# One more pair of tiles 2 to 17 computed as a split product, with a written order for the first phase and the first 24 tiles

## The chip, the cores and the metric

The kernel runs on one core of one Trainium2 chip. The metric is device time in microseconds, from one execution of the whole program; lower is better. TensorE does the matmuls, VectorE (DVE), ScalarE (ACT) and GpSimd (POOL) the elementwise work, and the queue of SyncE (SP) issues all the DMAs.

## The reference

Two batches of 12480 tokens with 128 channels, 49 agents, 2048 hidden units, all float32:

```python
agent_v = softmax(scale * agents @ k.T) @ v          # per batch, 49 x 128
x       = softmax(scale * q @ agents.T) @ agent_v    # per batch, 12480 x 128
h       = x @ w_in                                   # 24960 x 2048
g       = where(h >= 1, h, where(h <= -1, 0, (h + 1)**2 / 4))
out     = g @ w_out                                  # 24960 x 128
```

The product `agent_v @ w_in` is formed once for each batch, so `h` of a token is its 49 softmax weights times a 49 x 2048 matrix.

## The kernel before

**Tiles.** The 24960 tokens are cut into 49 tiles of 512 tokens (the last has 384). The 2048 hidden units of a tile are handled as 8 pairs of two blocks of 128. For each pair: `g1` (L2025, TensorE) computes `h` into PSUM (`ph`); ACT makes `relu(0.5 h + 0.5)` (L2033) and squares it (L2038); DVE forms `g = max(min(g, 1), h)` (`gate`, L2041).

**Second product.** `g @ w_out` is then done in one of two ways, by a letter per pair:
- N, a plain float32 pair: `g` is multiplied directly by the float32 weights (`g2n`, `total<-g,wo` at L2071).
- D, A or P, a split pair: `g` is rounded to a float32r tile `ghi` (the "hi" step, on DVE at L1089, ACT at L1085 or POOL at L1087), the rest `glo = g - ghi` is formed (the "lo" step, L2052, on DVE or POOL by a second letter), and three products are added: `ghi,wo_hi`, `ghi,wo_lo` and `glo,wo_hi`, all at L2071.

Both accumulate in two PSUM banks, `total0` and `total1`, one for each half of the rows. When all pairs of a tile are in, ACT copies bank 0 (`out`), DVE adds bank 1 (`join`, L2151), and SP stores the tile.

Tiles 0 to 17 have the letters `DPNPNDPP` / `PPDDDPDD` (two plain pairs, 2 and 4). Tiles 18 to 48 alternate `PPNPNDPP` / `PPPPDPDD` (two plain) and `PAPPNPDD` / `DDDPDDPP` (one plain).

**Queries.** For each tile (for two tiles together from tile 18 on) the scores `q @ agents` (L1879), their softmax (DVE and ACT; `pq` at L1912 is the last step), a transpose (`tr`, L1938) and two drains of it (`mc` on ACT at L1085, `ml` on DVE at L1948) make the small matrix `mt` that `g1` reads.

**First phase.** Before tile 0's second product, the keys and values of batch 0 are loaded and reduced, the weights are decoded from 64-bit words (L1176 to L1212) and `W` of batch 0 is formed. The keys of batch 1 (14 groups) are scored early into the banks `total0` and `total1` (L1128); each group is copied to `ks` by ACT or DVE and folded by DVE into a running maximum `top` (L1660), which ends in one reduction (L1691). Tile 0's second product needs these banks back. The values of batch 1 are weighted later, as riders on the query scores of tiles 5 to 12 (L1136; the subtraction is L1742 on POOL), and `W` of batch 1 is formed on those of tiles 13 to 17.

**Order.** A planner (`Order.run`) puts all steps into one order before the program is written out, with assumed durations; each engine then works through its own list in that order. Steps of the tiles have turns (tile number plus an entry of `TIMES`, `TIMES_2` or `PLAN`), and follow each other by turn on DVE, ACT and TensorE. `PLAN` has entries of their own for tiles 13 to 21 and 44 to 48; other tiles share `TIMES` (0 to 12) or the two of `TIMES_2`. The remaining steps (first phase, riders, DMAs, the queries of tiles 0 to 2) go greedily, whichever can start first, by a key; `FIRST` ranks 473 of them. Buffers limit it: three `ph` banks, five each of `g`, `ghi` and `glo`.

Of the kernel before, what the change touches and what calls it, by code (L numbers as in the profile page):

```python
# [11 lines left out]
AHEAD = 0.8  # L12
# [23 lines left out]

TIMES = dict(  # L40
    q=(-1.8875417,),
    mx=(-0.3865384,),
    sub=(-0.3146318,),
    exp=(-2.1729306,),
    tot=(0.1808175,),
    rec=(0.4518768,),
    norm=(0.4759488,),
    tr=(-0.1276526,),
    mc=(-1.0964621,),
    ml=(1.1333586,),  # L50
    out=(0.9032897,),
    join=(3.1102148,),
    g1=(0.0668635, 0.4000499, 0.1916538, 0.0411721, 0.8964628, 0.9435512, 0.9732315, 0.5142120),
    relu=(-0.5071955, -0.1941977, -0.4279925, -0.7025724, -0.0055905, 0.0340225, 0.2099995, -0.1183292),
    square=(-0.4804701, -0.1725691, -0.2858129, -0.5818398, 0.0945863, 0.1749406, 0.2375538, -0.0976778),
    gate=(1.6527569, 2.0147262, 1.9982946, 1.5815822, 2.2200233, 2.2700605, 2.5717267, 2.1086864),
    hi=(1.9175717, 2.5099120, None, 1.9817459, None, 2.5080745, 2.9293395, 2.4146834),
    lo=(2.3736696, 2.6831976, None, 1.9174717, None, 2.7685071, 2.6705867, 2.1491229),
    g2=(1.0521998, 1.5614394, 0.9499837, 1.0285587, 1.0875494, 1.4817716, 1.6962020, 0.9785378),
    g2l=(1.3136540, 1.7077630, None, 1.2353176, None, 1.8013004, 1.7208422, 1.3753477),  # L60
)

PAIRS = 18
QUERY = ("q", "mx", "sub", "exp", "tot", "rec", "norm")
HI_2 = ("PPNPNDPP", "PAPPNPDD")
LO_2 = ("PPPPDPDD", "DDDPDDPP")
TIMES_2 = (
    dict(  # L70
        q=(-1.5713,),
        mx=(-0.5974,),
        sub=(-0.5235,),
        exp=(-0.1685,),
        tot=(0.0236,),
        rec=(1.3849,),
        norm=(1.4461,),
        tr=(0.8994,),
        mc=(2.3488,),
        ml=(2.2710,),  # L80
        out=(4.4525,),
        join=(4.3718,),
        g1=(1.6621, 1.4877, 1.9336, 2.1986, 2.4419, 2.5160, 2.2733, 1.2761,),
        relu=(3.0360, 2.8721, 3.1890, 3.3281, 3.8045, 3.8312, 3.7296, 2.7669,),
        square=(3.3034, 3.1553, 3.3145, 3.3684, 3.8260, 3.9316, 3.7952, 2.8452,),
        gate=(3.1999, 3.0999, 3.2210, 3.2325, 3.4800, 3.7033, 3.3712, 2.7199,),
        hi=(62.3857, 62.0442, None, 62.5259, None, 3.7501, 62.7598, 61.8730,),
        lo=(62.6767, 62.2078, None, 62.7896, None, 62.8395, 3.7723, 3.1606,),
        g2=(2.7027, 2.4767, 2.5185, 2.8430, 2.8277, 3.0118, 2.9034, 2.5554,),
        g2l=(2.9002, 2.5015, None, 2.8840, None, 3.1268, 2.9103, 2.7007,),  # L90
    ),
    dict(
        tr=(1.2661,),
        mc=(2.6113,),
        ml=(2.2934,),
        out=(4.7847,),
        join=(4.3181,),
        g1=(2.2479, 1.8295, 1.5940, 1.5287, 2.4567, 2.1755, 1.8336, 1.7939,),
        relu=(3.6045, 3.1881, 3.0018, 2.9632, 3.8472, 3.5778, 3.2527, 3.1117,),
        square=(3.8312, 3.3162, 3.0897, 2.9701, 3.8503, 3.7077, 3.3291, 3.1391,),  # L100
        gate=(3.7103, 3.0976, 2.9045, 2.7898, 3.9433, 3.5896, 3.1374, 2.9799,),
        hi=(62.7859, 3.4148, 61.9105, 61.9524, None, 62.5856, 3.4494, 3.0235,),
        lo=(4.0405, 3.5378, 2.9935, 62.0055, None, 3.8415, 62.3033, 62.0323,),
        g2=(2.9416, 2.6801, 2.3409, 2.3085, 3.2104, 3.0125, 2.4289, 2.3251,),
        g2l=(3.2075, 2.6861, 2.4733, 2.4846, None, 3.2923, 3.3724, 2.6053,),
    ),
)
PLAN = {
    13: dict(
        q=(-1.8875,),  # L110
        mx=(-0.3303,),
        sub=(-0.2435,),
        exp=(-2.0215,),
        tot=(0.2512,),
        rec=(0.4553,),
        norm=(0.6044,),
        tr=(-0.1505,),
        mc=(-1.0807,),
        ml=(1.1437,),
        g1=(  # L120
            0.0661, 0.2927, 0.2186, 0.0309,
            0.8249, 0.8521, 1.0696, 0.5431,
        ),
        relu=(
            -0.5630, -0.3641, -0.4949, -0.7518,
            -0.0200, 0.1707, 0.3731, -0.1859,
        ),
        square=(
            -0.5050, -0.2158, -0.3273, -0.7210,
            0.1039, 0.3272, 0.3999, -0.1026,  # L130
        ),
        gate=(
            1.6537, 1.9476, 1.8362, 1.6224,
            2.1550, 2.4118, 2.5022, 2.0639,
        ),
        hi=(
            2.0137, 3.5040, None, 2.0680,
            None, 2.4627, 4.3563, 2.9470,
        ),
        lo=(  # L140
            2.5714, 3.5050, None, 1.7949,
            None, 3.9050, 2.8465, 2.4354,
        ),
        g2=(
            1.2684, 1.5254, 1.0404, 0.8654,
            1.1496, 1.7221, 1.4987, 1.0531,
        ),
        g2l=(
            1.4845, 1.6689, None, 1.4204,
            None, 1.9048, 1.8506, 1.5448,  # L150
        ),
        out=(0.9856,),
        join=(3.1582,),
    ),
    14: dict(
        q=(-1.8674,),
        mx=(-0.3313,),
        sub=(-0.2221,),
        exp=(-2.0994,),
        tot=(0.1109,),  # L160
        rec=(0.1722,),
        norm=(0.5086,),
        tr=(-0.1639,),
        mc=(-0.8055,),
        ml=(1.1705,),
        g1=(
            0.2526, 0.3343, 0.3675, 0.1185,
# [2138 lines left out]
```

## Time and profile before

| | |
|---|---|
| runs, us | 1011.97, 1012.07, 1012.99 (median 1012.07) |
| span of the profiled execution | 1011.9 us (no other time of that execution is recorded) |
| TensorE (PE) busy | 988.7 us, 98% |
| ACT busy | 909.4 us, 90% |
| DVE busy | 882.1 us, 87% |
| POOL busy | 720.9 us, 71% |
| DMA moved | 57.03 MB |
| chain that ended last | PE 78%, ACT 9%, DVE 5%, issue 3%, DMA 2% |

Busy shares are means over stages of different kinds. In the page's 40 slices of 25.3 us the DMA engines are at 90 to 100% in the first two and below 30% from the fourth on; PE reads 7 and 8 tenths in the first two slices, 8 in the last, and 9 or more in all between; TensorE's granted clock reads 9 tenths or more in every slice. The stages have to be read one by one.

### The profile page before, as it was taken

Reading aid. Unit: us, or ns where it says so; the run is one execution under the profiler, and the core shown is the slowest. Engines: PE = TensorE matmul, PEld = TensorE weight load, DVE = VectorE, ACT = ScalarE, POOL = GpSimd, SP = SyncE. Lnnn points to the kernel's source line nnn. Section 1 sums busy time; section 2 is a strip of 40 time slices with the busy share of each in tenths; the row PEclk is TensorE's granted clock in tenths of the full one; section 3 lists DMA queues with packets and bytes.
Section 4 is the critical chain, followed back from the end, with each engine's and each line's share of the span. In section 5 each row is a group of like instructions: output and inputs, shape, how many; then the busy total and the mean of one; then the engine's idle time right before and its main releaser. Section 6 shows DMA issues by size and latency. Waiting matters only on the chain.

```text
span 1011.9 us, 22370 instructions
## 1 busy us (share of the span) xinstructions
PE 988.7 (98%) x9143; PEld 757.3 (75%) x9143; DVE 882.1 (87%) x1008; ACT 909.4 (90%) x1008; POOL 720.9 (71%) x423
## 2 busy tenths in 40 slices
PE   7899999999999999999999999999999999999998
PEld 5767777777777676867778878778777877777777
DVE  7698988887899889889889889889989889988986
ACT  3488988888899889889999999999999999999996
POOL 3536766667566554777877887878878788788785
PEclk9999999999999999999999999999999999999999
DMA  9981021212000101000100100101011010000000
GB/s 352 401 315 37 23 69 59 69 59 68 23 26 29 33 22 43 33 32 12 43 32 12 43 32 12 43 32 35 20 32 42 12 33 30 12 22 12 11 22 19
DMA packets 23862, 57.03 MB, mean 56 GB/s; under 512 B 2768, under 2 KB 3280, under 8 KB 23760
## 3 DMA queue, kind: packets, MB, share of 16 engines
q1 hardware_dynamic: 23760, 55.60, 15.4%
q8 instruction: 72, 1.18, 0.5%
q14 instruction: 30, 0.25, 0.1%
HBM read 42.81 MB, written 12.78 MB: 55 GB/s over the span
## 4 chain that ended last, share of the span: by engine, by line
PE 78%; ACT 9%; DVE 5%; issue 3%; DMA 2%; POOL 1%; SPq 0%; DVEq 0%; ACTq 0%; POOLq 0%
PE total L2071 46%; PE ph L2025 24%; ACT g L2033 5%; ACT g L2038 3%; DVE g L2041 3%; PE ph L1879 3%; PE ph L1938 1%; PE ph L1136 1%; PE total L1136 1%; DMA kbuf<-kT 1%; PE total L2064 1%; DVE glo L2052 1%; DMA g<-kT 1%; DMA qt<-qT 1%; POOL glo L2052 1%
## 5 line engine op out<-in xcount | busy, mean ns | idle before, releaser
L2052 POOL TENSOR_TENSOR glo<-g,ghi 128x1024 fp32r<-128x1024 f32 (+1 forms) x163 | 429.9, 2643 | 155.9 <-DVE ghi L1089 114.6
L2041 DVE SCALAR_TENSOR_TENSOR g<-g,ph 128x1024 f32<-128x1024 f32 (+1 forms) x392 | 467.2, 1210 | 72.5 <-ACT g L2038 54.9
L2033 ACT ACTIVATE g<-ph,half 128x1024 f32<-128x1024 f32 (+1 forms) x392 | 427.8, 1104 | 45.1 <-PE ph L2025 38.5
L2038 ACT ACTIVATE g<-g 128x1024 f32<-128x1024 f32 (+1 forms) x392 | 406.5, 1054 | 6.1
L1087 POOL CAST ghi<-g 128x1024 fp32r<-128x1024 f32 (+1 forms) x212 | 253.9, 1216 | 89.9 <-DVE g L2041 82.2
L2025 PE MATMUL ph<-mt,w_hi 49*128 49x512 f32 (+2 forms) x1600 | 278.4, 420 | 6.7 <-DVE g L2041 6.3
L2071 PE MATMUL total<-ghi,wo_hi 64*128 64x512 f32 x1212 | 198.7, 397 | 0.0
L2025 PEld LDWEIGHTS ph<-mt,w_hi 49*128 49x128 f32 x1600 | 146.7, 185 | 68.4 <-issue 25.4
L2052 DVE TENSOR_TENSOR glo<-g,ghi 128x1024 fp32r<-128x1024 f32 (+1 forms) x146 | 192.8, 1321 | 4.3 <-POOL ghi L1087 2.6
L2071 PE MATMUL total<-ghi,wo_lo 64*128 64x512 f32 x1212 | 195.2, 392 | 0.0
L2071 PE MATMUL total<-glo,wo_hi 64*128 64x512 f32 x1212 | 179.7, 397 | 0.0
L2025 PE MATMUL ph<-mt,w_lo 49*128 49x512 f32 (+2 forms) x800 | 160.9, 386 | 0.0
L2071 PE MATMUL total<-g,wo 64*128 64x512 f32 x648 | 153.8, 589 | 1.4 <-DVE top L1660 1.4
L2071 PEld LDWEIGHTS total<-ghi,wo_hi 64*128 64x128 f32 x1212 | 120.9, 185 | 23.8 <-issue 2.3
L2071 PEld LDWEIGHTS total<-ghi,wo_lo 64*128 64x128 f32 x1212 | 121.1, 184 | 21.7
L2071 PEld LDWEIGHTS total<-glo,wo_hi 64*128 64x128 f32 x1212 | 117.4, 185 | 22.4 <-issue 1.2
L2071 PEld LDWEIGHTS total<-g,wo 64*128 64x128 f32 x648 | 65.2, 185 | 44.0 <-issue 36.8
L2025 PEld LDWEIGHTS ph<-mt,w_lo 49*128 49x128 f32 x800 | 79.6, 185 | 13.9 <-DVE w_lo L1550 0.2
L1089 DVE CAST ghi<-g 128x1024 fp32r<-128x1024 f32 x82 | 66.4, 810 | 1.5
L1879 PEld LDWEIGHTS ph<-ag,qt 128*64 128x64 f32 x780 | 25.7, 137 | 19.7 <-issue 13.1
L2151 DVE TENSOR_TENSOR ot<-ot,total 128x512 f32<-128x512 f32 x48 | 32.8, 684 | 6.8 <-ACT ot L1085 6.5
L1085 ACT ACTIVATE ot<-total 128x512 f32<-128x512 f32 (+1 forms) x49 | 28.6, 585 | 9.6 <-PE total L2064 5.1
(120 smaller groups left out, 559.2 us busy)
## 6 DMA issues: line engine op xcount, KB each, us to landing
qt<-qT SPq DMA_DIRECT2D x48, 256.0 KB, 2.8
outT<-ot SPq DMA_DIRECT2D x48, 256.0 KB, 2.0
vbuf<-v_in SPq DMA_DIRECT2D x18, 451.5 KB, 4.6
kbuf<-kT SPq DMA_DIRECT2D x17, 448.0 KB, 7.5
ghi<-v_in SPq DMA_DIRECT2D x5, 451.5 KB, 8.1
glo<-v_in SPq DMA_DIRECT2D x5, 451.5 KB, 8.1
g<-kT SPq DMA_DIRECT2D x5, 448.0 KB, 9.2
raw<-w_in SPq DMA_DIRECT2D x4, 512.0 KB, 7.0
```

What stands on the lines that cost most here:

```text
L1085: act.activation(out=out, in_=in_, func=ACTF.Copy)
L1087: pool.tensor_copy(out, in_)
L1089: dve.tensor_copy(out, in_)
L1136: nc.tensor.matmul(out=ps[c:c + 64, 0:C + 1], lhsT=ksf[:, g, t * A:t * A + 64], rhs=vt[:, t, :], start=n + t < 2, stop=n + t >= m - 2,)
L1879: nc.tensor.matmul(out=ps[c, m * A:(m + 1) * A], lhsT=st["q", x][:, i * 128:][:, c], rhs=ag[:, b, :], start=True, stop=True,)
L2025: nc.tensor.matmul(out=st["h"][:, c, lo:hi], lhsT=W[b][w][r, f:f + 128], rhs=M[j][r, x, lo:hi], start=(i == 0), stop=(i == 2),)
L2033: act.activation(out=st["g"], in_=st["h"][:, :, 0:n], func=ACTF.Relu, bias=half, scale=0.5)
L2038: act.activation(out=st["g"], in_=st["g"], func=ACTF.Square)
L2041: dve.scalar_tensor_tensor(out=st["g"], in0=st["g"], scalar=1.0, in1=st["h"][:, :, 0:n], op0=ALU.min, op1=ALU.max,)
L2052: (pool if e == "POOL" else dve).tensor_tensor(out=st["lo"], in0=st["g"], in1=st["hi"].bitcast(F32), op=ALU.subtract)
L2071: nc.tensor.matmul(out=tot[i][:, 0:n], lhsT=w[r, f, :], rhs=x[r, c, :], start=begins, stop=LEFT[j] == 0,)
L2151: dve.tensor_tensor(out=st["o"], in0=st["o"], in1=tot[1][:, 0:n], op=ALU.add)
```

## The change

Every step now has a turn, and each engine's list is sorted by turn alone: the planner no longer picks greedily, it only works out the waits. `PLAN` has an entry for each of the 49 tiles, with the query loads (`ld`) and the stores (`st`) in it; `LEAD` gives turns to the 386 steps of the first phase and of the riders; nine of these move to their second engine (`SECOND`). The turns of tiles 24 to 48 put these tiles' steps in the same sequence on TensorE, ACT, DVE and POOL as before.

The letters stand per tile. Pair 4 of tiles 2 to 17 is split instead of plain. Over these 16 tiles the hi steps go from 32 DVE, 64 POOL, 0 ACT to 31 DVE, 70 POOL, 11 ACT, and the lo steps from 48 DVE, 48 POOL to 61 DVE, 51 POOL. Five drains `mc` (tiles 6, 7, 10, 14, 15) and one `out` (tile 12) go from ACT to DVE. Tile 0 has one lo step on DVE and five on POOL instead of three and three; tile 1 has three hi steps on DVE instead of two. Tiles 19, 20, 21 and 23 have one or two letters changed, and the same number of plain pairs.

In the first phase's DMA list, the loads of the keys of batch 0 all stand ahead of its values, with three weight loads and one query load between them (before, two loads of values stood among the keys).

```diff
-HI_ENG = (("DPNPNDPP",), ("DPNPNDPP",))
-LO_ENG = (("PPDDDPDD",), ("PPDDDPDD",))
+CUT = ('DPNPNDPP', 'DPNDNDPP', 'DPNPPDPP', 'DPNAPAPP', 'PDNPPPAD', 'DPNPDPAP', 'PDNPDPPP', ...
+LOW = ('PPDPDPPD', 'PPDDDPDD', 'PPDDDPDD', 'PPDDDPDD', 'PPDDDPDD', 'PPDDDPDD', 'PPDDDPDD', ...
+MC_ON = 'AAAAAADDAADAAADDAAAADAAAAAAAAAAAAAAAAAAAAAAAAAAAA'
+OUT_ON = 'AAAAAAAAAAAADAAAAAAAAADAAAAAAAAAAAAAAAAAAAAAAAAAA'
...
+    def settle(self):
+        rest = [op for op in self.ops if op.turn is None]
+        for op, turn in zip(rest, LEAD):
+            op.turn = turn
+        for i in SECOND:
+            rest[i].choices = rest[i].choices[1:]
...
     def run(self):
+        self.settle()
+        queues = {
+            e: sorted(
+                (op for op in self.ops if op.choices[0][0] == e),
+                key=lambda op: (op.turn, op.n), reverse=True,
+            )
+            for e in self.ENGINES
+        }
...
-            x = add(("ACT", 0.5), hi, [d], k)
-            y = add(("ACT", 0.3), keep, [d], k)
-            wo_ops.append(add(("POOL", 1.3, 1), lo, [x, y], k, (), ((b, d),)))
+            x = add(("ACT", 0.8), hi, [d])
+            wo_ops.append(add(("POOL", 1.3, 1), lo, [x], (), (("wf", d),)))
...
-            x = step("mc", ("ACT", 0.08 + n / 1.2e3), mc, [tr_op], j=j)
+            x = step("mc", drain(MC_ON, j, n), mc, [tr_op], j=j)
```

The rest of the diff renames steps, removes switches that had one setting, shortens the `ks` buffer and the zeroing of its tail, and changes two waits that the planner assumes for DMAs.

## Rows read from the trace of the kernel before

**Rows 1.** Windows: stretch, its length, busy us (instructions) PE, PEld, DVE, ACT, POOL; clock, DMA.

```profile
51.00:78.50 27.50, 23.80 (x444) 17.23 (x444) 27.08 (x47) 23.14 (x36) 11.65 (x10) 1.00 0.80 297
...
116.00:438.00 322.00, 318.71 (x2770) 238.72 (x2769) 282.56 (x334) 287.97 (x315) 202.77 (x125) 1.00 0.13 43
438.00:576.00 138.00, 135.47 (x1222) 105.56 (x1220) 122.21 (x125) 131.75 (x139) 107.16 (x60) 1.00 0.09 30
576.00:997.00 421.00, 420.58 (x3650) 325.71 (x3647) 377.33 (x386) 407.03 (x434) 341.69 (x184) 1.00 0.07 25
```

**Rows 2.** Waits of PE, 78.5 to 560 us: total us, times, longest.

```profile
PE ph L2025 <- DVE g L2041: 5.8, 15, 0.9
```

**Rows 3.** Timeline of PE, 651 to 666 us: start, us, engine line op xcount.

```profile
651.39 0.64 PE L2071 MATMUL total<-ghi,wo_hi 64*128 64x512 f32 x4
...
655.13 0.64 PE L2025 MATMUL ph<-mt,w_hi 49*128 49x512 f32 x4
...
663.88 1.90 PE L2071 MATMUL total<-g,wo 64*128 64x512 f32 x8
665.60 0.54 PE L1938 MATMUL ph<-ident,pq 64*113 64x64 f32 x8
```

**Rows 4.** Instruction groups by form, 116 to 438 us: busy, mean ns, idle before.

```profile
L2038 ACT ACTIVATE g<-g 128x1024 f32<-128x1024 f32 x126 | 131.7, 1057 | 2.4
...
L2052 DVE TENSOR_TENSOR glo<-g,ghi 128x1024 fp32r<-128x1024 f32 x47 | 68.6, 1461 | 2.0 <-POOL ghi L1087 0.9 <-PE total L2071 0.8
L1089 DVE CAST ghi<-g 128x1024 fp32r<-128x1024 f32 x31 | 21.6, 695 | 0.1
L1948 DVE TENSOR_TENSOR mt<-ph,mt 113x512 fp32r<-113x512 f32 x16 | 10.9, 682 | 0.3 <-ACT mt L1085 0.3
...
L1912 DVE TENSOR_TENSOR pq<-qd,qsm 128x392 f32<-128x392 f32 x14 | 8.3, 589 | 0.3
...
L2052 POOL TENSOR_TENSOR glo<-g,ghi 128x1024 fp32r<-128x1024 f32 x48 | 125.7, 2621 | 86.7 <-DVE ghi L1089 77.2 <-PE total L2071 7.4 <-PE ph L2025 1.0
L1087 POOL CAST ghi<-g 128x1024 fp32r<-128x1024 f32 x65 | 70.6, 1111 | 34.3 <-DVE g L2041 31.0 <-PE ph L2025 3.3
L1742 POOL TENSOR_TENSOR ks<-ks,mb 128x343 f32<-128x343 f32 x12 | 10.3, 878 | 0.0
```

**Rows 5.** Timelines of POOL and DVE, 220 to 234 us.

```profile
220.16 2.02 POOL L1087 CAST ghi<-g 128x1024 fp32r<-128x1024 f32 x2 [1.84 <-DVE g L2041]
222.26 3.27 POOL L2052 TENSOR_TENSOR glo<-g,ghi 128x1024 fp32r<-128x1024 f32 x1
227.16 2.38 POOL L2052 TENSOR_TENSOR glo<-g,ghi 128x1024 fp32r<-128x1024 f32 x1 [1.63 <-DVE ghi L1089]
...
221.23 2.02 DVE L2052 TENSOR_TENSOR glo<-g,ghi 128x1024 fp32r<-128x1024 f32 x1
...
233.57 1.22 DVE L2052 TENSOR_TENSOR glo<-g,ghi 128x1024 fp32r<-128x1024 f32 x1
```

**Rows 6.** Instruction groups by form of POOL and DVE, 620 to 860 us.

```profile
L2052 POOL TENSOR_TENSOR glo<-g,ghi 128x1024 fp32r<-128x1024 f32 x45 | 119.0, 2650 | 21.7 <-DVE ghi L1089 12.0 <-PE total L2071 9.2
L1087 POOL CAST ghi<-g 128x1024 fp32r<-128x1024 f32 x60 | 79.0, 1329 | 22.1 <-DVE g L2041 20.7
...
L2052 DVE TENSOR_TENSOR glo<-g,ghi 128x1024 fp32r<-128x1024 f32 x39 | 47.5, 1217 | 0.0
L1089 DVE CAST ghi<-g 128x1024 fp32r<-128x1024 f32 x18 | 16.2, 900 | 0.6
```

**Rows 7.** Timelines of DVE, then PE, in the first phase.

```profile
67.56 1.30 DVE L2052 TENSOR_TENSOR glo<-g,ghi 128x1024 fp32r<-128x1024 f32 x1
...
77.39 0.50 DVE L1089 COPY ks<-total 128x343 f32<-128x343 f32 x1
...
36.01 0.60 PE L1136 MATMUL total<-ghi,ks 128*64 128x129 f32 x6 [1.93 <-issue]
...
78.47 1.95 PE L2071 MATMUL total<-g,wo 64*128 64x512 f32 x7 [1.44 <-DVE top L1660]
```

More of the change, by code (lines that the diff above doesn't have):

```diff
@@ L799, with __init__ @@
 class Op:
-    def __init__(self, order, choices, fn, deps, key, acq, rel):
-        self.choices, self.fn, self.deps, self.key = choices, fn, list(deps), key
+    def __init__(self, n, choices, fn, deps, acq, rel):
+        self.n, self.choices, self.fn, self.deps = n, choices, fn, list(deps)
         self.acq, self.rel = acq, rel
-        self.n = order
-        self.start = self.end = None
+        self.start = self.end = self.engine = None
         self.slots = {}
@@ new lines, in earliest @@
+                at = max(at, stored[op.tile - 1][1] if op.tile else 0.0)
+            if op.reads in seen and seen[op.reads][0] != e:
+                x, end = seen[op.reads]
+                at = max(at, end + latency(x, e))
+            return at
+        while any(queues.values()):
+            best = None
+            for n, queue in enumerate(queues.values()):
+                if not queue:
+                    continue
+                at = earliest(queue[-1])
+                if at is None:
+                    continue
+                e, us, shared = queue[-1].choices[0]
+                c = max(at, free[e], port if shared else 0.0), n, queue
+                if best is None or c[:2] < best[:2]:
+                    best = c
+            assert best is not None, [q[-1].tag for q in queues.values() if q]
+            at, _, queue = best
+            op = queue.pop()
+            e, us, shared = op.choices[0]
@@ L1025, in agent_attention_moe @@
     wo_lo = const.tile([128, NC, 128], F32R, name="wo_lo")
+    native = sorted({p for table in CUT for p in range(NP) if table[p] == "N"})
+    wo = {p: const.tile([128, 2, 128], F32, name=f"wo{p}") for p in native}
     def width(j):
@@ L1485, in keys_phase @@
                 else:
-                    last = add(("DVE", 0.55), halves, [x], k + 1)
+                    last = add(("DVE", 0.55), halves, [x])
         return last, av_ops[1:]
-    W, FORMS = {}, []
+    W = {}
     def plus(ps):
@@ L1524, in n3 @@
             ]
-        x = add(("PE", 0.32), n2, [acc_op], key + 0.1)
+        x = add(("PE", 0.32), n2, [acc_op])
         back = take(x)
-        nx = add(("DVE", 0.2), n3, [x], key + 0.2)
-        r = add(("DVE", 0.26), n1, [nx], key + 0.25, (), (back,))
+        nx = add(("DVE", 0.2), n3, [x])
+        r = add(("DVE", 0.26), n1, [nx], (), (back,))
         done = []
@@ L1553, in lo @@
                 )
-            x = add(("PE", 0.87), form, [nx, win_ops[i]], key + 0.3 + i, ("h",))
-            FORMS.append(x)
-            y = add(("ACT", 0.5), hi, [x, r], key + 1 + i)
-            done.append(add(("DVE", 0.6), lo, [y], key + 1.1 + i, (), (("h", x),)))
+            x = add(("PE", 0.87), form, [nx, win_ops[i]], ("h",))
+            y = add(("ACT", 0.5), hi, [x, r])
+            done.append(add(("DVE", 0.6), lo, [y], (), (("h", x),)))
         return done
@@ L1676, in early @@
             KE[g] = add(
-                (("ACT", 0.355), ("DVE", 0.42)), evac, [y, wait[g]], key + 0.1, (),
+                (("ACT", 0.355), ("DVE", 0.42)), evac, [y, wait[g]], (),
                 () if g and g not in GMP1 else ((lent, x),),
@@ L2119, in pair, with last @@
             x.rows = y.rows = 256
-        SECOND.setdefault(j, []).extend((x, y))
-    def last_g1(j):
-        return max(range(NP), key=lambda p: time("g1", j, p))
-    def last(j, n, *turns):
+        PRODUCTS.setdefault(j, []).extend((x, y))
+    def last(j, n):
         for i, e in enumerate(("ACT", "DVE")):
@@ L2135, in store @@
                 nc.sync.dma_start(out=outT[:, at:at + n // 2], in_=st["o"])
-            x = add((e, 0.06 + n / 1.92e3), evac, SECOND[j], turns[i] * NP, ("o",))
-            x.turn, x.tag = turns[i], (("out", "join")[i], j, 0)
+            x = timed(
+                add((e, 0.06 + n / 1.92e3), evac, PRODUCTS[j], ("o",)), ("out", "join")[i], j
+            )
             x.store = j if i else None
-            load(64 * n * 4, store, [x], turns[i] * NP, (), (("o", x),))
+            timed(load(64 * n * 4, store, [x], (), (("o", x),)), "st", j)
     def output(j):
```

2104 lines of the change are left out of this document (1184 added, 920 removed), and 68 rows, old and new, of tables (FIRST, LEAD).

## The prediction

> **What bounds the kernel now.** Start with the page's shares: TensorE is busy 98% of the span, so the first question is where the other 2% lie, and a mean cannot tell. The table of windows by stage does [rows 1]. From 576 to 997 us PE is busy 420.58 of 421 us: nothing but less TensorE work can shorten that stretch. From 116 to 438 us, in which the outputs of the 16 tiles 2 to 17 end, it is busy 318.71 of 322, and from 438 to 576 us 135.47 of 138. From 51 to 78.5 us PE has slack (23.80 of 27.50), and DVE has none (27.08). So the kernel has two bounds: DVE in the second half of the first phase, TensorE from then on. The list of waits names the TensorE idle behind 78.5 us: 15 waits for `gate`, the DVE step that turns `h` into `g`, 5.8 us in all [rows 2], which is what the two middle windows lack (3.3 + 2.5).
>
> **TensorE: what one more split pair is worth.** In the PE timeline [rows 3] eight groups of four split-product matmuls fill 651.39 to 655.13 us, 0.4675 us for a group. A split pair is three such groups (`ghi,wo_hi`, `ghi,wo_lo`, `glo,wo_hi`): 1.40 us. A plain pair is one row of eight records, 663.88 to 665.60: 1.72 us. Each exchange takes 0.32 us off TensorE, and there are 16: 5.1 us. All of it is on the path as long as PE stays fed, since PE is busy 99% of that stretch [rows 1]. I take -5.1 us; the ends are 0 (it all comes back as waits) and 5.1.
>
> **What the split adds on the other engines.** The 16 new hi steps and 16 new lo steps, with the letters moved, make per engine over tiles 2 to 17:
> - DVE: 13 more lo steps, one hi step less, six drains more. An unblocked lo step is 1.22 us [rows 5], a hi step 0.70, a drain about the 0.68 of `mt` [rows 4]: 15.9 - 0.7 + 4.1 = 19.3 us.
> - ACT: 11 hi steps at the 1.06 of the square, which has the same shape [rows 4]: 11.7 us, less the six drains that leave it.
> - POOL: 3 lo steps at 2.38 and 6 hi steps at 1.01 [rows 5]: 13.2 us.
>
> The stretch would last 322 - 5.1 = 317 us. DVE goes from 282.6 to 301.9 us, 95%; without the time that its lo steps now spend blocked (47 times 1.461 - 1.22, 11.3 us [rows 4]) it is 290.6, 92%. ACT goes to at most 299.7, 95%. POOL, 202.8 + 13.2, has room. In the stretch from 576 to 997 us ACT is at 407.03 of 421, 97%, DVE at 90%, with PE idle 0.4 us [rows 1]: ACT's level has been carried before, DVE's has not quite.
>
> **The two engines are not independent.** POOL's two casts run from 220.16 to 222.18, and the DVE lo step that starts at 221.23 takes 2.02 us instead of 1.22; the POOL lo step behind it starts at 222.26 and takes 3.27 instead of 2.38 [rows 5]. In each case the later one ends about its own length after the earlier one has ended. So I add up these steps as if only one could run at a time. Before, 116 to 438 us [rows 4]: POOL 48 x 2.38 + 65 x 1.01 + 12 x 0.88, DVE 47 x 1.22 + 31 x 0.70 + 14 x 0.59 = 190.5 + 87.3 = 277.8 us, 86% of 322. After: 13 x 1.22 + 3 x 2.38 + 6 x 1.01 - 0.70 = 28.4 us more, 306.2 of 317, 97%. The check is the later stage, 620 to 860 us [rows 6]: 45 x 2.38 + 60 x 1.01 + 39 x 1.22 + 18 x 0.70 = 227.9 of 240, 95% before the query products are counted, while PE does not wait. There POOL takes the blocked time (lo 2650 ns, hi 1329) and DVE's lo steps hardly any (1217).
>
> The Trainium skill has this as a rule ("SBUF — State Buffer", section "Who interferes with whom"): a DVE instruction with two SBUF inputs, or in a two-port mode, contends with GpSimd instructions that read SBUF, and whichever issues first holds the pair for the whole instruction while the other blocks. The rows above agree. By that rule alone every added lo step speaks against the change; what it makes of the time is the third rival below.
>
> **Hand-over and waits.** The new order has its own turns for every tile, so the 5.8 us of waits for `gate` can go or grow. In tiles 18 to 23 (2.5 us, 438 to 576) only the order and five letters change, and no TensorE work: the window behind it shows that two-tile patterns of these letters run without a wait, so I take -2.0 there. In tiles 2 to 17 (3.3 us) better turns pull one way and 92 to 95% on DVE the other: I take 0, with -3.3 and +5 (an extra 0.3 us for each tile, the size of one wait of rows 2, 5.8/15 = 0.39) as ends. Where a wait goes, the next late thing there is the same `gate`: behind it stand the lo steps of DVE's list, and the following `g1` that needs its `ph` bank.
>
> **First phase.** DVE runs without a gap from 51 us until the last key group of batch 1 is folded; TensorE's first second-product, at 78.47 us, waits 1.44 us for exactly that [rows 7]. Out of the DVE list before this point go one lo step of tile 0 (1.22 of the row's 1.30, as the rows beside it overlap) and one of three copies of `ks` (0.50, about 0.42 to the next start; ACT has 4.4 us free there [rows 1]). That moves the release 1.6 us earlier. The two lo steps moved to POOL, 2 x 2.38, fall in its 15.9 idle us of 27.5 [rows 1]. Ahead of 51 us, PE idles 1.93 us before the weighting of the values resumes at 36.01 [rows 7]; key loads ahead of all value loads could win that, while a 512 KB weight load now ahead of the last two key loads could cost some 1.3 us (an estimate, at the 401 GB/s that the page's second slice reads). I take -1.6 for the phase, with -3.6 and +1.0 as ends. The merged copy of the plain weights issues the same instructions; the shorter zeroing of `ks` lies under the first loads: nothing for either. Stores and query loads share SP's list by turn; a late store would hold a query load behind it, but its turn is two tiles or more ahead of its own tile's store, so nothing; if that cover went, the price for a tile is one load's landing, 2.8 us by the page's part 6.
>
> **Sum.** -5.1 - 2.0 + 0 - 1.6 = -8.7 us. The profiled span is 1011.9 us, 0.2 under the median of the runs, 1012.07; from the median it gives 1003.4 us. From tile 24 on all lists are in the same sequence, so nothing is expected back there.
>
> **Rivals.**
> 1. TensorE's saving comes back as waits. For: DVE at 92 to 95% with riders that come in bursts. Against: PE waits for it only 3.3 us in 322 now, at 88%. Only the first phase gains: 1012.1 - 1.6 = 1010.5 us (1007.5 to 1012.5).
> 2. More than the sum: all 5.8 us of waits go and the first phase gains 3.6: 1012.1 - 5.1 - 5.8 - 3.6 = 997.6 us. For: 0.4 us idle in 421 later. Against: the riders make no two tiles alike here.
> 3. Slower. POOL's longest hold is one lo step, 2.38 us. DVE now has 322 - 282.6 = 39 us free in 16 tiles, 2.5 a tile; after, 317 - 301.9 = 15 us, 0.9 a tile. If the denser order puts one more DVE lo step or cast of each tile behind a whole POOL lo step, DVE falls 2.38 - 0.9 = 1.5 us short per tile, `gate` is late by that, and PE, with three `ph` banks, stops: 16 x 1.5 = 24 us, or 1003.4 + 24 = 1027 us. It decides from 0.9 us more blocking per tile; slower than before from 1.5 (0.9 + 8.7/16). For: the total is 97% of the stretch. Against: the later stage at 95% and more shows DVE's lo steps unblocked.
>
> The rule cited above, taken with the sums above, gives this third case if every conflict falls on DVE, and the forecast if POOL takes them as it does after 620 us.
>
> **Chances.** Forecast 0.66 (997.5 to 1007.5), rival 1 0.18, rival 2 0.05, rival 3 0.11. About 0.2% (2 us) is what a measurement of this kernel can tell from no change. Faster by more: forecast, rival 2 and half of rival 1, 0.80. Within it: the other half and a mild form of rival 3, 0.10. Slower: 0.10. The range runs from 997.5 to 1011.5, which leaves out part of rival 1, rival 2's lower half and rival 3, not quite 2 in 10.
>
> **What the profile after would show.** Split pairs at 1.40 us where the plain ones of pair 4 were, and PE busy some 5 us less in tiles 2 to 17; the last fold into `top` about 1.6 us earlier, and the first second-product with it; waits for `gate` from 78 to 560 us at 2 to 6 us. Wrong: waits for `gate` over 9 us, DVE lo steps in tiles 2 to 17 well over 1461 ns on average, a first second-product later than 78.5 us, or a changed period behind tile 24.

## The result and the profile after

The changed kernel takes 1018.94 us (median of 4 runs, 1015.13 to 1021.02) against 1012.31 (4 runs): a ratio of 1.0061 [1.004, 1.0081]. It is slower by 6.6 us, where 8.7 us less was forecast. Its runs spread over 5.9 us, those of before over 1.0, and the spread belongs to the result: the shortest run has a mean granted clock of 0.998, the other three 0.992 to 0.995. The profile is of the shortest run (span 1013.3 us).

From the page: busy time by engine, the chain that ended last by engine, and the plain products.

```profile
PE 982.9 (97%) x9200; PEld 769.5 (76%) x9200; DVE 911.7 (90%) x1033; ACT 915.4 (90%) x1013; POOL 756.3 (75%) x425
...
PE 75%; DVE 11%; ACT 8%; issue 4%; POOL 1%; DMA 0%; DVEq 0%; POOLq 0%; ACTq 0%
...
L2407 PE MATMUL total<-g,wo 64*128 64x512 f32 x520 | 125.3, 595 | 0.1
```

PE has 5.8 us less to do, and DVE's share of the chain has gone from 5% to 11%. The windows of [rows 1], after the change:

```profile
51.00:78.50 27.50, 24.88 (x440) 18.45 (x440) 26.81 (x43) 24.96 (x37) 18.02 (x12) 1.00 0.59 217
116.00:438.00 322.00, 311.17 (x2786) 241.01 (x2783) 304.47 (x346) 291.00 (x316) 233.75 (x130) 0.99 0.15 49
438.00:576.00 138.00, 135.51 (x1238) 109.84 (x1236) 125.60 (x128) 130.72 (x138) 107.86 (x59) 1.00 0.09 30
576.00:997.00 421.00, 420.58 (x3656) 330.00 (x3654) 377.66 (x386) 407.30 (x434) 342.01 (x184) 1.00 0.07 25
```

The last stretch is as it was. The second has TensorE idle for 10.8 of 322 us instead of 3.3. The waits of PE from 78.5 to 560 us name the cause by the line of [rows 2]:

```profile
PE ph L2361 <- DVE g L2377: 14.1, 17, 1.7
```

Two more waits than before, but 8.3 us more: some have become long. Groups by form, 116 to 438 us, to set beside [rows 4]:

```profile
L2388 POOL TENSOR_TENSOR glo<-g,ghi 128x1024 fp32r<-128x1024 f32 x50 | 136.0, 2722 | 46.4 <-DVE ghi L1446 25.0 <-ACT ghi L1442 8.8 <-PE total L2407 7.4
L2388 DVE TENSOR_TENSOR glo<-g,ghi 128x1024 fp32r<-128x1024 f32 x60 | 90.3, 1511 | 0.1
L1444 POOL CAST ghi<-g 128x1024 fp32r<-128x1024 f32 x68 | 88.1, 1306 | 41.9 <-DVE g L2377 25.5 <-PE total L2407 11.3 <-PE ph L2361 2.9
L1446 DVE CAST ghi<-g 128x1024 fp32r<-128x1024 f32 x30 | 23.5, 790 | 0.0
L2257 DVE TENSOR_TENSOR pq<-qd,qsm 128x392 f32<-128x392 f32 x14 | 12.2, 875 | 0.0
```

The mean DVE lo step rose only from 1461 to 1511 ns. The mean hides the cause; the timelines show it. POOL, then DVE, then PE, around the longest wait, the place of [rows 5]:

```profile
219.82 2.02 POOL L1444 CAST ghi<-g 128x1024 fp32r<-128x1024 f32 x2 [1.18 <-DVE g L2377]
221.93 2.58 POOL L2388 TENSOR_TENSOR glo<-g,ghi 128x1024 fp32r<-128x1024 f32 x1
...
221.47 0.79 DVE L2257 TENSOR_TENSOR pq<-qd,qsm 128x392 f32<-128x392 f32 x1
222.19 3.41 DVE L2388 TENSOR_TENSOR glo<-g,ghi 128x1024 fp32r<-128x1024 f32 x1
225.52 2.34 DVE L2377 SCALAR_TENSOR_TENSOR g<-g,ph 128x1024 f32<-128x1024 f32 x2
...
223.96 0.63 PE L2407 MATMUL total<-ghi,wo_hi 64*128 64x512 f32 x4
224.42 0.63 PE L2407 MATMUL total<-ghi,wo_lo 64*128 64x512 f32 x4
226.78 0.74 PE L2361 MATMUL ph<-mt,w_hi 49*128 49x512 f32 x4 [1.73 <-DVE g L2377]
```

POOL starts its lo step 0.26 us ahead of DVE's. DVE's step then takes 3.41 us instead of 1.22, the gate behind it starts 2.2 us late, and TensorE stands 1.73 us. The same pattern, POOL ahead by 0.0 to 0.35 us and a DVE lo step or cast of 2.95 to 3.43 us, stands in front of PE's waits at 99.68, 120.84, 285.18 (there some gates further back), 437.42 and 502.46 us. The six waits make 8.8 of the 14.1 us. In all six the planner's order has the DVE step first. Nothing on the chip holds that order: the two steps belong to different pairs, and no semaphore joins them. From 78 to 560 us the profile of before has one DVE lo step of that length (3.07 us at 376.43), and the next wait of TensorE behind it is 0.52 us.

Another wait, 1.01 us at 176.01 behind a blocked `pq` (1.65 us), has a second price. Windows of 4 us of the same kernel:

```profile
172.00:176.00 4.00, 3.01 (x32) 2.44 (x29) 4.00 (x5) 2.95 (x5) 1.18 (x1) 1.00 0.00 0
176.00:180.00 4.00, 3.82 (x18) 2.37 (x20) 3.97 (x5) 2.65 (x3) 2.79 (x3) 0.71 0.40 129
180.00:184.00 4.00, 4.00 (x30) 2.99 (x28) 3.19 (x4) 3.21 (x4) 2.48 (x1) 0.87 0.89 299
```

Behind the wait the granted clock reads 0.71 and 0.87 of 2.4 GHz; a plain row of eight matmuls at 178.13 takes 3.37 us where the one of [rows 3] takes 1.90. In clock alone that is (0.29 + 0.13) x 4 = 1.7 us. Behind 40 us, the profile of before has no 4 us slice under 0.97.

In this profile the first phase is shorter. The reduction of `top` starts at 75.08 us instead of 78.35; the timelines of DVE (before, then after) and PE (after; before in [rows 7]):

```profile
78.35 0.79 DVE L1691 TENSOR_REDUCE pm<-top 128x49 f32<-128x343 f32 x1
...
75.08 0.79 DVE L2039 TENSOR_REDUCE pm<-top 128x49 f32<-128x343 f32 x1
...
75.19 1.95 PE L2407 MATMUL total<-g,wo 64*128 64x512 f32 x7
```

Not all of these 3.3 us belong to the change. The copy `avT` stands about halfway through the phase. It comes at 51.03 us before and at 48.95 after, but some of the runs below have the first phase of one kernel or the other unchanged, and there it moves. Copy and reduction in e8 (first phase of before), in the changed kernel, and in e4 (first phase of the changed kernel):

```profile
49.70 0.29 DVE L1521 COPY avT<-ph 128x128 f32<-128x128 f32 x1 [0.78 <-PE ph L1501]
77.02 0.79 DVE L1691 TENSOR_REDUCE pm<-top 128x49 f32<-128x343 f32 x1
...
48.95 0.29 DVE L1875 COPY avT<-ph 128x128 f32<-128x128 f32 x1 [0.77 <-PE ph L1855]
...
52.47 0.29 DVE L1886 COPY avT<-ph 128x128 f32<-128x128 f32 x1 [0.77 <-PE ph L1866]
78.58 0.79 DVE L2050 TENSOR_REDUCE pm<-top 128x49 f32<-128x343 f32 x1
```

From the copy to the reduction it is 27.3 us before and in e8, and 26.1 in the changed kernel, e2, e4 and e10. So 1.2 us are gained there, and the other 2.1 are within what one run differs from the next.

A ruler for the rest is DVE's join, once a tile. Tile 0 and tile 23, before, then after (timelines of DVE):

```profile
97.75 0.68 DVE L2151 TENSOR_TENSOR ot<-ot,total 128x512 f32<-128x512 f32 x1
557.84 0.69 DVE L2151 TENSOR_TENSOR ot<-ot,total 128x512 f32<-128x512 f32 x1 [0.68 <-ACT ot L1085]
```

```profile
93.36 0.68 DVE L2477 TENSOR_TENSOR ot<-ot,total 128x512 f32<-128x512 f32 x1
559.43 0.69 DVE L2477 TENSOR_TENSOR ot<-ot,total 128x512 f32<-128x512 f32 x1 [0.69 <-ACT ot L1442]
```

From tile 0 to tile 23: 460.1 us before, 466.1 after. Tiles 1 to 23 lost 6.0 us, with 5.1 us less to compute.

### The profile page after: what moved, and what is told of

The parts are those of the page before. It is cut to its first block, busy times and chain, and to the rows that moved or that the text cites. A ratio compares the mean times of both kernels' runs of the same rounds, so it can differ in the third digit from the quotient of the medians.

```text
span 1013.3 us, 22547 instructions
## 1 busy us (share of the span) xinstructions
PE 982.9 (97%) x9200; PEld 769.5 (76%) x9200; DVE 911.7 (90%) x1033; ACT 915.4 (90%) x1013; POOL 756.3 (75%) x425
## 4 chain that ended last, share of the span: by engine, by line
PE 75%; DVE 11%; ACT 8%; issue 4%; POOL 1%; DMA 0%; DVEq 0%; POOLq 0%; ACTq 0%
PE total L2407 44%; PE ph L2361 23%; ACT g L2369 4%; DVE g L2377 4%; ACT g L2374 3%; PE ph L2224 2%; DVE glo L2388 2%; PE ph L2279 1%; PE total L2400 1%; DVE pq L2257 1%; PE ph L1493 1%; POOL glo L2388 1%; DVE ghi L1446 1%; PE total L1493 1%; PE total L1485 0%
## 5 line engine op out<-in xcount | busy, mean ns | idle before, releaser
L2388 POOL TENSOR_TENSOR glo<-g,ghi 128x1024 fp32r<-128x1024 f32 (+1 forms) x169 | 449.2, 2662 | 117.6 <-DVE ghi L1446 66.5
L1444 POOL CAST ghi<-g 128x1024 fp32r<-128x1024 f32 (+1 forms) x215 | 271.3, 1274 | 94.2 <-DVE g L2377 71.5
L2388 DVE TENSOR_TENSOR glo<-g,ghi 128x1024 fp32r<-128x1024 f32 x156 | 209.9, 1348 | 0.4 <-POOL ghi L1444 0.3
L2407 PE MATMUL total<-ghi,wo_hi 64*128 64x512 f32 x1276 | 209.0, 398 | 0.1
L2407 PE MATMUL total<-ghi,wo_lo 64*128 64x512 f32 x1276 | 204.9, 392 | 0.0
L2407 PE MATMUL total<-glo,wo_hi 64*128 64x512 f32 x1276 | 196.1, 398 | 0.0
L2407 PE MATMUL total<-g,wo 64*128 64x512 f32 x520 | 125.3, 595 | 0.1
L2407 PEld LDWEIGHTS total<-g,wo 64*128 64x128 f32 x520 | 53.5, 188 | 34.7 <-issue 29.5
L1446 DVE CAST ghi<-g 128x1024 fp32r<-128x1024 f32 (+1 forms) x83 | 70.6, 855 | 1.9 <-PE total L2407 0.8
L1442 ACT ACTIVATE ot<-total 128x512 f32<-128x512 f32 (+1 forms) x47 | 27.5, 585 | 10.0 <-PE total L2400 5.1
L2279 PEld LDWEIGHTS ph<-ident,pq 64*113 64x113 f32 x390 | 28.2, 174 | 8.9 <-issue 4.9
```

The source lines that it names most:

```text
L1442: act.activation(out=out, in_=in_, func=ACTF.Copy)
L1444: pool.tensor_copy(out, in_)
L1446: dve.tensor_copy(out, in_)
L2279: nc.tensor.transpose(ps[0:R, h, i * 64:i * 64 + 64], pq[r, i].rearrange("p x a -> p (x a)")[:, 0:R], ident[r, r],)
L2388: (pool if e == "POOL" else dve).tensor_tensor(out=st["lo"], in0=st["g"], in1=st["hi"].bitcast(F32), op=ALU.subtract)
L2407: nc.tensor.matmul(out=tot[i][:, 0:n], lhsT=w[r, f, :], rhs=x[r, c, :], start=begins, stop=LEFT[j] == 0,)
```

## The experiments

The theory: unenforced order between POOL's and DVE's SBUF steps delays gates, and the clock falls behind some of the waits. Its rivals: DVE is simply too full; the turns are bad in themselves; the clock falls by chance. Each kernel was timed beside runs of the kernel before (medians 1012.51 to 1012.85), and ratios are against these.

**e1_port_order.** In the six places POOL's lo step first reads one column of what the DVE step writes, so that it cannot start ahead of it: the step is held. (In the expectations lo 1.7 is the lo step of tile 1, pair 7.)

```diff
+BEHIND = {
+    ("lo", 1, 1): ("lo", 1, 7), ("lo", 2, 1): ("lo", 2, 7), ("lo", 7, 1): ("lo", 7, 7),
...
+            if ("lo", j, p) in BEHIND:
+                x = WROTE[BEHIND["lo", j, p]]
+                pool.tensor_copy(seen_x, x[:, 0, 0:1].bitcast(F32))
             (pool if e == "POOL" else dve).tensor_tensor(
```

> The changed kernel, with six POOL lo steps each made to read one element of a DVE result first, so that they start behind the DVE lo or hi step that the planner had ahead of them (lo 1.1 behind lo 1.7, lo 2.1 behind lo 2.7, lo 7.1 behind lo 7.7, lo 10.3 behind lo 9.6, lo 17.5 behind lo 17.4, lo 21.3 behind hi 21.7). Theory A, the order in which the two engines meet: these six DVE steps fall from 3.0 to 3.4 us to 1.2 us, the waits of TensorE behind them (1.64, 1.68, 1.73, 0.87, 1.64, 1.25, together 8.8 us) go, and the span falls from 1013.3 to about 1005, with times within 2 us of each other. Theory B, the load as such is too high for DVE, POOL and ACT: the waits turn up at other gates, the total of waits for gate stays above 9 us and the span above 1010.

1007.73 us, 0.9948 [0.9936, 0.996]: faster than before, 11.2 us below the changed kernel. The runs lie within 4.3 us, not 2. POOL, then DVE, at the place shown above:

```profile
224.25 0.19 POOL L2397 COPY seen_x<-glo 128x1 f32<-128x1 f32 x1 [1.61 <-DVE glo L2398]
224.39 2.42 POOL L2398 TENSOR_TENSOR glo<-g,ghi 128x1024 fp32r<-128x1024 f32 x1
...
222.97 1.21 DVE L2398 TENSOR_TENSOR glo<-g,ghi 128x1024 fp32r<-128x1024 f32 x1
224.11 2.34 DVE L2383 SCALAR_TENSOR_TENSOR g<-g,ph 128x1024 f32<-128x1024 f32 x2
```

The waits of PE, 78.5 to 560 us:

```profile
PE ph L2367 <- DVE g L2383: 5.1, 9, 1.6
```

Neither step is blocked: DVE's takes 1.21 us, POOL's 2.42. From tile 0 to tile 23 it is 453.9 us (joins at 99.28 and 553.20), 6.2 less than before. None of the six waits is left; the longest that is, 1.57 us at 401.67, stands behind a DVE lo step that a POOL cast held for 0.9 us.

Letters, turns and DVE's work are those of the changed kernel. So neither a DVE that is too full nor the turns by themselves made the six waits.

**e10_read_only.** The control: the same six reads, behind POOL's step and of its own result.

```diff
+READ = (('lo', 1, 1), ('lo', 2, 1), ('lo', 7, 1), ('lo', 10, 3), ('lo', 17, 5), ('lo', 21, 3))
...
                 out=st["lo"], in0=st["g"], in1=st["hi"].bitcast(F32), op=ALU.subtract
             )
+            if ("lo", j, p) in READ:
+                pool.tensor_copy(seen_x, st["lo"][:, 0, 0:1].bitcast(F32))
```

> The changed kernel with the six added reads of one column that e1 has, but behind the six POOL lo steps instead of ahead of them, and of the step's own result: the same number of instructions, and nothing is held back. Theory (e1 won by the order of the two engines' steps): no gain, 1017 to 1020 us, with TensorE's waits for gate at 12 to 15 us and the blocked DVE steps of 3.2 to 3.4 us still there. Rival (any small shift of POOL's list undoes the accidents): 1006 to 1012 us, waits under 8 us.

1017.54 us, 1.0051 [1.0036, 1.0065]; waits for `gate` 14.1 us, tile 0 to 23 again 466.1 us, and the DVE steps of 3.1 to 3.4 us are all there. The added instructions do nothing; the order does it.

**e12_three_holds.** Only the holds in tiles 1, 2 and 7 (the edit against e1).

```diff
 BEHIND = {
     ("lo", 1, 1): ("lo", 1, 7), ("lo", 2, 1): ("lo", 2, 7), ("lo", 7, 1): ("lo", 7, 7),
-    ("lo", 10, 3): ("lo", 9, 6), ("lo", 17, 5): ("lo", 17, 4), ("lo", 21, 3): ("cut", 21, 7),
 }
```

> The changed kernel with three of e1's six holds (POOL's lo steps of tiles 1, 2 and 7); those of tiles 10, 17 and 21 start as in the changed kernel. Theory (each blocked DVE step costs its own wait, and some runs a fall of the clock behind it): waits for gate 8 to 10 us, about half of e1's 11.2 us come back, median 1011 to 1015 us, still with clocks of 0.992 to 0.998. Rival (one of the six makes the whole loss): 1007 to 1009 us, or no gain, 1017 to 1020 us.

Waits 9.7 us, as expected; tile 0 to 23 in 459.3 us, 6.8 of the 12.2 us that all six holds give (in both the clock's 1.7 at 176 to 184 us is among them, which did not fall there). The median is 1015.38, 1.0022 [1.0012, 1.0032], a little above the expected range: in the profile tile 0 ended at 100.1 us, with the clock at 0.54, 0.50 and 0.68 from 72 to 84 us, and seven of eight runs have a mean clock of 0.992 or 0.993. So the loss adds up over the places; no single one makes it.

**e4_gates_first.** The six DVE steps moved behind the next gates in DVE's own list, with no hold.

```diff
+MOVED = {
+    ('lo', 1, 7): ('gate', 1, 5),
+    ('lo', 2, 7): ('gate', 2, 5),
...
+        n, i, m = MOVED.get((name, j, p), (name, j, p))
+        o.turn, o.tag = i + PLAN[i][n][m], (name, j, p)
```

> The changed kernel with the same six DVE steps moved behind the next one to three gate steps of DVE's list, no letter and no other step touched. Theory A: the gates no longer stand behind a blocked DVE step, the six waits go, and the span is about 1005 to 1007 us. Theory B: the lo steps, now later, make the second product wait instead, and the span stays above 1010.

1018.61 us, 1.0061 [1.0043, 1.0079]: nothing won. Instead of six DVE lo steps and casts of 2.9 us and more there are two (291.96, 500.25), but the waits for `gate` of `g1` fall only to 11.1 us; all waits of TensorE from 78.5 to 560 us together are 14.9 us, against 14.6 in the changed kernel. They stand at other places (128.52, 231.68, 445.71 and more), and not all of them behind a blocked step: ahead of the wait of 1.47 us at 523.42 DVE stood 2.02 us for a POOL cast. Reordering one list moved the waits; what makes each of the new ones was not tested.

**e11_lo_on_pool.** For the rival that DVE is too full: one lo step in each of the tiles 2 to 17 moved from DVE to POOL.

```diff
+MORE = ((2, 3), (3, 4), (4, 4), (5, 4), (6, 4), (7, 4), (8, 4), (9, 4), (10, 2), (11, 2), ...
+LOW = tuple("".join("P" if (j, p) in MORE else x for p, x in enumerate(c)) for j, c in enumerate(LOW))
```

> The changed kernel with one lo step of each of the tiles 2 to 17 moved from DVE to POOL (pair 4 in ten tiles, pair 3 or 2 in the others), turns unchanged. DVE loses 16 x 1.22 = 19.5 us and falls to some 285 us of 322, about what it had before the change; POOL gains 16 x 2.38 = 38 us and has 320 - 234 = 86 free. Rival to the theory (DVE at 95% is simply too full): TensorE's waits for gate fall under 8 us and the median is 1006 to 1013 us. Theory (the two engines' steps hold each other up, and a lo step holds for 2.38 us on POOL against 1.22 on DVE): waits do not fall, 14 us or more, median 1018 to 1035 us.

1071.73 us, 1.058 [1.0566, 1.0593], worse than either theory gave. DVE was busy 268 of 322 us (83%), less than before the change, and PE waited far more, 78.5 to 560 us:

```profile
PE ph L2364 <- DVE g L2380: 30.3, 15, 7.1
PE total L2410 <- POOL glo L2391: 6.8, 3, 3.4
```

Freeing DVE did not help. But this run changes more than DVE's load. In its profile the granted clock alone makes some 31 us (what it lacks of 1.00, summed over 4 us windows from 40 to 996 us; 1.7 in the changed kernel): the many waits drew many falls. And ACT waits 31.8 us, in eight places, for POOL's lo steps to give a `g` buffer back (0.7 in the changed kernel). How much of the rest is the longer hold and how much are turns that were written for other letters, it does not tell; against a DVE that is too full the evidence is e1.

**e3_order_only.** Pair 4 plain again, the order as changed.

```diff
+CUT = tuple(c[:4] + "N" + c[5:] if 2 <= j < 18 else c for j, c in enumerate(CUT))
```

> The changed kernel with pair 4 of tiles 2 to 17 plain again, all else as changed: the order and the other letters alone. TensorE has 5.1 us more work. Theory A: lo 1.7, 2.7, 7.7 and 9.6 are still there and still fall behind whole POOL lo steps, waits for gate stay at 6 us or more, span about 1015. Theory B: with four to five per cent less on DVE and POOL the waits for gate fall below 5 us and the clock does not fall: 1013.3 + 5.1 - 9 - 2, about 1008.

1063.74 us, 1.0522 [1.0496, 1.0548]; 27.5 us of waits for `gate`, and some 29 us of granted clock, summed as in e11. It missed both ways: ACT waits 44.0 us, in eleven places, for a second product to give a `g` buffer back (1.5 us in the changed kernel), which fits a pair 4 that keeps the late turn of a split pair. It does not separate letters from order; it only shows that the turns do not fit these letters. The split alone on before's order was not tried on the chip.

**e2_fill.** The changed kernel with matmuls that add nothing in six of the waits.

```diff
+KEEP = {(2, 3): 6, (3, 3): 6, (8, 3): 6, (18, 2): 6}
+KEEP_TR = {6: 7, 17: 12}
...
+            for i in range(KEEP.get((j, p), 0)):
+                for c in range(2):
+                    r = slice(64 * c, 64 * c + 64)
+                    nc.tensor.matmul(
+                        out=tot[c], lhsT=idle[r, 0:128], rhs=idle[r], start=False, stop=False
+                    )
             st["h"] = new_h()
```

> The changed kernel, with matmuls of zeros put into six of TensorE's waits for gate (before g1 of tile 2, 3, 8 and 18, and behind the transposes for tiles 6 and 17); they add nothing to any result. Theory C, part of the loss is the TensorE clock, which falls after such a wait: the granted clock is 1.00 in every stretch behind the start, the runs lie within 1 us of each other, and the time is that of the changed kernel's best run less about 2 us, 1012 to 1013 us (the waits themselves stay, filled). If the spread of 1015 to 1021 us has another cause, the runs spread by 4 us or more as before.

1017.47 us, 1.0047 [1.0035, 1.0059], clocks 0.993 to 0.999, spread 4.4 us: theory C missed on all three. The profile has no fall at 176 us any more, but one at 284 to 288 (0.57), behind a wait of 0.88 us that was not filled. The loss stays, since the gates stay late; for the clock it is suggestive, no more.

**e8_late_gates.** Waits of known place in the kernel before: three more DVE steps ahead of one gate in five steady tiles.

```diff
         def gate(o, e):
+            if p == 5 and j in (29, 32, 35, 38, 41):
+                for i in range(3):
+                    dve.tensor_scalar(vbuf[i], vbuf[i], 1.0, None, ALU.min)
```

> The kernel before, with three added DVE steps of about 0.6 us each (a tile of values of batch 0 is multiplied by nothing new; the output stays) ahead of the gate of pair 5 in tiles 29, 32, 35, 38 and 41, a stretch in which TensorE otherwise never waits. It makes five waits of known place. Theory (a wait of about 1.5 us costs its own length and, in part of the runs, a fall of the clock behind it): TensorE waits 5 x 1 to 1.8 us there, the median rises by the sum of the waits plus up to 2.5 us for each fall, 1018 to 1030 us, with the granted clock at 0.6 to 0.9 in slices of 4 us right behind some of the waits and a spread over 2 us. Rival (waits cost their length alone): the clock stays at 1.00 behind all of them and the rise is the sum of the waits within 0.5 us, with a spread under 1 us.

1031.2 us (1026.21 to 1033.48), 1.0176 [1.0154, 1.0198]. The steps took 1.30 us each, not 0.6, and three of the waits were 3.0 us, two 0.81. The waits of PE, 560 to 1026 us, in the profiled run:

```profile
PE ph L2025 <- DVE g L2044: 11.8, 8, 3.0
```

That run has a mean clock of 1.000 and shows no fall; at 1026.21 us it is 13.7 above the median of before, the waits and 1.9 more. The other four have 0.990 to 0.997 and take 2.3 to 7.3 us longer with the same program. In the profiled run the waits cost about their length and drew no fall. That the others lost their time to falls behind these waits fits their mean clocks, but no profile of them shows the place: the theory's profile reading failed here, its spread did not.

**e5_port_fold, e6_port_fill, e9_port_fold_fill.** e1 still has runs at 0.993; its profile shows a 1.65 us wait for `top` at 71.41 us (in the changed kernel at 69.80; timelines of PE, the changed kernel first) and, behind it, the windows:

```profile
69.80 1.84 PE L1485 MATMUL total<-ag,kbuf 128*64 128x49 f32 x56 [1.66 <-DVE top L2008]
...
71.41 1.99 PE L1491 MATMUL total<-ag,kbuf 128*64 128x49 f32 x56 [1.65 <-DVE top L2014]
```

```profile
72.00:76.00 4.00, 4.00 (x70) 3.16 (x68) 3.26 (x4) 2.66 (x4) 1.82 (x3) 0.62 0.01 4
76.00:80.00 4.00, 4.00 (x28) 2.95 (x26) 3.23 (x5) 3.47 (x5) 3.57 (x4) 0.50 0.00 0
80.00:84.00 4.00, 4.00 (x18) 2.05 (x16) 2.52 (x3) 1.50 (x2) 2.47 (x1) 0.60 0.00 0
```

e5 moves two folds ahead in DVE's list and so shortens that wait; e6 fills the waits that e1 has left; e9 does both.

```diff
+EARLIER = {295: -1.35342, 300: -1.35341}
...
+KEEP = {(8, 2): 2}
+KEEP_OWN = {(0, 7): 5}
+KEEP_TR = {6: 7, 17: 12}
```

> The kernel of e1 (six POOL steps held behind DVE) with two folds of the first phase's maximum moved ahead of a gate of tile 0 in DVE's list, so that TensorE's 1.65 us wait for the maximum at 71.4 us gets shorter. Theory (what is left of e1's loss is the granted clock, which falls to 0.57 behind such waits, and not the waits themselves): the wait is about 0.5 us, the clock between 72 and 84 us stays at 1.00, tile 0 ends near 93.4 us instead of 99.3, and the median is 1003 to 1005 us. Rival (the wait has nothing to do with the clock, the fall comes by chance in any stretch): clocks spread as in e1, 0.993 to 0.998, and the median stays at 1006 to 1008 us.

> The kernel of e1 with matmuls on an idle tile (they add nothing to the output) placed where TensorE still waits: five ahead of a g1 of tile 0, four ahead of one of tile 8, 7 and 12 ahead of the transposes of tiles 6 and 17. The waits stay as long as they were, only filled. Theory (the clock falls because TensorE stands still): the mean clock is 0.998 or more in all runs, the spread is under 1.5 us, and the median is 1003 to 1005 us. Rival (the clock falls by chance, whether TensorE works there or not): clocks 0.993 to 0.998 as in e1, median 1006 to 1008 us, or later where the fillers delay real work.

> The kernel of e1 with the edits of e5 and e6 together. Theory (the clock falls behind unfilled waits): all runs at 0.998 or more, median 1002 to 1004 us, spread under 1.5 us, the best version. Rival (falls by chance): no better than e1, 1006 to 1008 us.

e5: 1005.72 us (1003.08 to 1008.92), 0.9932 [0.9917, 0.9947]. The median is a little above the expected range. The wait is 0.53 us (with two more of 0.50 and 0.43 behind it), 72 to 84 us stay at 1.00, but the clock falls behind an unfilled wait of 1.00 us at 173.97 (0.57 from 176 to 180), and the runs still spread, not by clock alone: two runs with a mean clock of 0.997 are 2.4 us apart.

e6: 1004.34 us (1004.20 to 1005.13), 0.9917 [0.9905, 0.993], clocks 0.998 to 1.000: median, clock and spread as the theory had them. The same windows, and the waits from 78.5 to 560 us:

```profile
72.00:76.00 4.00, 3.99 (x94) 3.43 (x96) 3.94 (x6) 3.57 (x6) 1.84 (x2) 1.00 0.02 4
76.00:80.00 4.00, 3.90 (x28) 2.49 (x26) 3.93 (x6) 3.97 (x5) 4.00 (x4) 1.00 0.00 0
80.00:84.00 4.00, 4.00 (x40) 3.26 (x36) 3.67 (x5) 3.30 (x4) 3.58 (x3) 1.00 0.00 0
```

```profile
PE ph L2386 <- DVE g L2402: 2.5, 9, 0.6
```

The filled gates come no earlier: tile 0 to 23 takes 453.9 us as in e1. What the filling gives back is the clock, 3.4 us in the median (the mean clocks of the two, 0.995 and 0.999, are 0.0034 apart, which is 3.4 us of 1005). e9: 1004.83 us (1003.08 to 1006.73), 0.9922 [0.9909, 0.9935], no better than e6 within the intervals and not the best version, as its theory had it; its clocks are 0.998 to 1.000, but its runs spread over 3.7 us. Tile 0 to 23 takes 454.1 us there too, and tile 0 ends at 96.97 us, so in its profile the difference lies in the first phase. e6 has the lowest median of all that was run: 8.2 us under the kernel before, 14.6 under the changed one.

## Why the prediction was wrong

- **TensorE, -5.1: right.** The split groups in the timeline above start 0.46 us apart, plain matmul records fall from 648 to 520 (16 pairs x 8), and PE's busy time from 988.7 to 982.9 us.
- **Hand-over and waits, -2.0 and 0: the step that failed.** Tiles 1 to 23 lost 6.0 us with 5.1 less to compute, a loss of 11.1 us where the forecast took a gain of 2.0. Waits for `gate` are 8.3 of it (14.1 us instead of 5.8, where 2 to 6 were forecast), the clock 1.7; some 1 us is not placed. The step took it for granted that the two engines' steps meet in the planner's order, or that POOL takes the blocked time as it does after 620 us; in six places DVE took it, and holding POOL there (e1) gives 12.2 us back over these tiles, the clock's 1.7 among them. My upper end of +5 was taken from the size of waits that were there (0.39 us each); the new kind, DVE behind a whole POOL lo step, is 0.9 to 1.7 us each.
- **The third rival named this mechanism**, with its mark (waits over 9 us), and got 0.11; its price, 24 us for one such step in each of 16 tiles, was too high, since it struck in six places in 23 tiles. I dismissed it by a sum, 97% of the stretch, and by a later stage at 95% where DVE's lo steps are hardly blocked (its casts were: 900 ns there, against 0.70 us [rows 4, rows 6]). A sum cannot answer it: e1 carries the same sum with 5.1 us of waits. The rows around 222 us show that with POOL 0.26 us ahead DVE loses 2.2 us, and with POOL held behind it 0.0. The rule that I cited says it (the Trainium skill, "SBUF — State Buffer", section "Who interferes with whom": it is issue order that decides who blocks), and e1 against e10 agrees, with 9.8 us between them. I used it for how long a block is and not for who comes first. That the later stage does well because it repeats one two-tile pattern, while the 24 tiles with turns of their own meet the question anew in each, is my reading; no run tested it.
- **The clock was missing.** I wrote down 1.00 from every window and no term for its falling. The profiled run is only 1.4 us longer in span than before; its terms: first phase -3.3, TensorE -5.1, waits +8.3, clock +1.7, in all +1.6. The median is 3.8 us longer still, and the three longer runs have mean clocks of 0.992 to 0.995 against 0.998: by 0.003 of 1015 us, 3 us of it would be clock (an estimate; these runs have no profile), and the first phase can make the rest, which is not shown. Behind 40 us, every fall in the profiles stands at a wait of 0.87 us or more, and e6 and e9, without such waits, have none. But most such waits pass without a fall: of nine in the changed kernel's profile from 52 us on one drew one, and the three of 3.0 us in e8 drew none. The same wait for `top`, 1.65 or 1.66 us, drew one in four profiles (e1, e3, e11, e12) and none in four (the changed kernel, e2, e4, e10). So no fall is seen without a wait, and whether a wait draws one differs from run to run; what decides it is open. The Trainium skill ("TensorE: Matmul & The Clock Gate", section "What's actually happening") says that the clock follows how busy TensorE has been recently. e6 against e1 agrees; which of the waits draws a fall no row here tells.
- **First phase, -1.6: near, and 2.1 us of luck in the profile.** `top` was ready 3.3 us earlier in the profiled run, but only the 1.2 us between the copy of `avT` and the reduction are there in every profile without a clock fall in that stretch; this is the part that the sum priced, DVE's list. That the keys going first gained anything ahead of 51 us is not shown: with the changed first phase `avT` is copied between 48.95 and 52.47 us (e2, e4, e10 and the changed kernel), with that of before at 49.70 and 51.03. From the reduction to the end of tile 0 another 1.1 us is gained, steadily too, which no term had.
- **Tail: right.** From 576 to 997 us PE is busy 420.58 us in both.

With the order held (e1, e6), tiles 1 to 23 take 6.2 us less than before, near the 5.1 + 2.0 of the forecast, and e6's 1004.34 us lies 0.9 above the predicted time. The sum was that of the planner's order; the chip ran another. That e6 comes so close is partly luck: it has holds and filled waits that the forecast did not know, and tile 0's 1.1 us, which no term had, makes up for the 0.9 that tiles 1 to 23 gained less.

## What to carry to other kernels

Where two engines can block each other on SBUF and no semaphore orders them, a written order is only a wish: list the pairs of steps that start within half a microsecond of each other, and price the wrong winner of each, not the sum of their times. A one-column read of the other's result (0.19 us on POOL) makes the order hold. Count with it that a TensorE wait of a microsecond can cost more than its length in some of the runs, and look at the spread of runs and the granted clock before reading a median.

## What the hardware showed beyond expectation

- A wait of 1.65 us in the first phase was followed by 12 us at 0.50 to 0.62 of the full clock (e1), as low as the 1.2 GHz level, and tile 0 ended 99.28 us into the span against 93.36 in the changed kernel's profile: 5.9 us. Of these, 1.6 were there already ahead of the fall (the same wait ends at 71.41 us instead of 69.80), so the fall cost 4.3 us, 2.6 times the wait itself.
- Matmuls whose result is not used, put into a wait, made the kernel faster (e6 against e1: 3.4 us in the median, and a spread of 0.9 us instead of 4.3; e9, filled as well, spreads over 3.7).
- A gate, which reads one operand from PSUM, ran at its usual length beside POOL's lo step (2.34 us for two at 224.11 in e1, while POOL's step ran from 224.39 on): the steps held for 2 us and more were DVE's lo steps, which read two operands from SBUF, and a cast from SBUF to SBUF (2.95 us at 497.10 in the changed kernel).
